# Attention over channels, then a two-layer MLP: from a schedule chosen by the compiler to one pipeline in written order

## The chip, the cores and the metric

The kernel runs on one core of one Trainium2 chip. The metric is the time of the program on the device in microseconds (us), median of several executions. TensorE has two clock levels, 1.2 and 2.4 GHz; the profile gives the granted clock as a share of the higher one. Engines are named as in the profile: PE (TensorE, with PEld for its weight loads), ACT (ScalarE), DVE (VectorE), POOL (GpSimd) and SP (SyncE, which only issues DMAs here).

## The reference

q, k and v are fp32 of shape (4, 6080, 256): four batches of 6080 tokens with 256 channels. Attention is over channels, so that its matrix is 256 x 256 for each batch; the result goes through a two-layer MLP with 2048 hidden units. tau is 1.

```python
def _attn_ref(q, k, v, tau):
    qn = q / (np.linalg.norm(q, axis=1, keepdims=True) + 1e-06)
    kn = k / (np.linalg.norm(k, axis=1, keepdims=True) + 1e-06)
    s = kn.transpose(0, 2, 1) @ qn / tau
    a = np.exp(s - s.max(-1, keepdims=True))
    a /= a.sum(-1, keepdims=True) + 1e-09
    return v @ a

def _moe_ref(x, w_in, w_out, s, b):
    r = np.maximum(x @ w_in, 0.0)
    g = s * (r * r) + b
    return g @ w_out
```

## The kernel before

**The gram.** For each batch the kernel needs the matrix k'q summed over 6080 tokens, and the sums of squares of q and k. `gram_chunks` (L104) cuts the tokens into six chunks of 1024 (the last 960). A chunk's q and k come by two DMAs from POOL's queue (L127, L131), cast from fp32 to fp16 on the way; partition p holds rows p, p+128 and so on, in runs of 1 KB in memory. ACT squares 2048 elements at a time (L147, L148), DVE folds the squares (L153 to L163), and PE adds 16 products of 256 columns to one PSUM bank (L167).

**The finish.** `gram_finish` (L178) turns the sums into norms (L180 to L190, with a reciprocal on 512 columns), scales the scores, takes the softmax (L201 to L222), transposes it (L228) and multiplies it into w_in (L237, L244). What comes out, wa16, takes v straight to the hidden layer, so that attention costs no pass of its own.

**The stream.** The 24320 tokens are cut into 48 groups of 512 (the last has 256; three groups straddle two batches). `stream_prep` (L264) loads v by POOL's queue and transposes it with eight PE transposes (L274) and a DVE copy (L278). `stream_moe` (L281) runs 16 steps m: two first-layer products of 512 columns into one of four h_ps banks (L311), a relu on ACT (L320), a square on DVE (L322), and, three steps later, four second-layer products of 256 columns into o_ps (L295), two PSUM banks that exist once. o_ps is cleared by DVE (L287) and evicted in one operation of 1024 columns (L330), which adds rowconst, the share of b, from 16 fp32 products (L99). The output leaves by SP's queue (L338).

**The order.** Nothing is pinned: the compiler's scheduler orders each engine's instructions by its own estimate of when they are ready, within what data and buffers allow. The main loop (L366) writes one chunk of the next batch's gram after each group, and the finish after the last chunk. SP loads both weights in fp32 at the start (L85, L90), ACT casts them (L87, L92). Buffers: three for a chunk's q and k, four for v, one for o_ps, four for h_ps, one more PSUM bank (ps_x) for everything else.

## Time and profile before

| | us |
|---|---|
| median of 3 runs | 905.42 |
| lowest and highest run | 902.81, 905.54 |
| span of the profiled execution | 900.5 |
| what the median has beyond that span | 4.9 |
| TensorE's recorded work in the span | 794.0 |
| VectorE's | 541.6 |
| ScalarE's | 558.2 |

The span goes from the first to the last instruction of one profiled execution. No time beside the span is recorded for that execution itself, so sums are made against the span, and the 4.9 us stand for what lies around it. In the timeline a row is one instruction, or several of a kind in a row (xN); the second number is the time from the start of the first to the end of the last, and matmuls overlap, so the pace of TensorE is read from start to start. In brackets stands the idle time ahead of the row and what ended it.

### The profile page before, as it was taken

To read this page: it belongs to the slowest core of one execution; us is meant where nothing else is said; L and a number is where in the kernel's file an instruction comes from. 1 tells how busy PE (TensorE), PEld (TensorE's weight loads), DVE (VectorE), ACT (ScalarE), POOL (GpSimd) and SP (SyncE) were. 2 spreads that over 40 slices of the span, in tenths; PEclk is the share of its full clock that TensorE was granted. 3 is DMA by queue.
4 is the path that set the end of the run, shared out by engine and by line. 5 is a ranking of instruction groups with operands and counts; after the bars stand their busy time and mean duration, and the time that the engine had idled before them with its cause. 6 is when DMAs were issued, how large, how long until landed. Compare 5 with 4: busy or idle time off the path is not lost.

```text
span 900.5 us, 14352 instructions
## 1 busy us (share of the span) xinstructions
PE 794.0 (88%) x5564; PEld 526.9 (59%) x5564; DVE 541.6 (60%) x1111; ACT 558.2 (62%) x893; POOL 85.7 (10%) x114
## 2 busy tenths in 40 slices
PE   0534799999998998778999899889999999999998
PEld 0313566666565665555566666556656666666666
DVE  1445486665766765455856676555665776565665
ACT  2864885666774655456776465556676565665665
POOL 4331300000001011111000101100000000000000
PEclk9976999999999999999999999999999999999999
DMA  9996951323026136566121713631212423230111
GB/s 230 198 197 85 197 92 36 72 38 69 24 60 105 36 71 98 80 94 94 31 48 47 107 36 69 102 62 36 60 25 47 75 44 59 48 66 25 47 41 43
DMA packets 102181, 67.38 MB, mean 75 GB/s; under 512 B 2528, under 2 KB 101856, under 8 KB 101856
## 3 DMA queue, kind: packets, MB, share of 16 engines
q0 software_dynamic: 74688, 37.36, 32.5%
q1 hardware_dynamic: 27424, 29.10, 10.1%
q8 instruction: 43, 0.70, 0.3%
q14 instruction: 26, 0.21, 0.1%
HBM read 78.91 MB, written 24.90 MB: 115 GB/s over the span
## 4 chain that ended last, share of the span: by engine, by line
PE 42%; issue 8%; DVE 4%; DMA 4%; ACT 1%; POOL 0%; ACTq 0%; POOLq 0%
PE o_ps L295 21%; PE h_ps L311 19%; DMA qc<-in_q_dram 3%; DMA kc<-in_k_dram 1%; DVE g L322 1%; ACT r L320 1%; PE vT_ps L274 1%; PE s_ps L167 1%; DVE o_sb L330 1%; DVE nrm L190 1%; PE wa_ps L237 1%; DVE o_ps L287 1%; DVE h_ps L307 0%; ACT sq L148 0%; DVE vT L278 0%
## 5 line engine op out<-in xcount | busy, mean ns | idle before, releaser
L320 ACT ACTIVATE r<-h_ps 128x512 f16<-128x512 f32 (+1 forms) x768 | 424.2, 601 | 248.1 <-PE h_ps L311 232.9
L295 PE MATMUL o_ps<-w_out,g 128*128 128x256 f16 x3040 | 426.5, 276 | 33.6 <-DVE g L322 32.8
L322 DVE TENSOR_TENSOR g<-r 128x512 f16<-128x512 f16 (+1 forms) x768 | 302.2, 418 | 223.1 <-ACT r L320 218.7
L311 PE MATMUL h_ps<-vT,wa 128*128 128x512 f16 (+7 forms) x1632 | 421.3, 370 | 0.3 <-DVE h_ps L307 0.2
L295 PEld LDWEIGHTS <-g 128*128 128x128 f16 x3040 | 290.1, 99 | 185.3 <-DVE g L322 54.9
L311 PEld LDWEIGHTS <-wa 128*128 128x128 f16 x1632 | 157.6, 99 | 83.7 <-issue 4.0
L267 POOL DMA_DIRECT2D v<-in_v_dram x48 | 36.2, 755 | 518.9 <-PE vT_ps L274 485.0
L167 PE MATMUL s_ps<-qc,kc 128*128 128x256 f16 (+1 forms) x384 | 58.4, 311 | 29.0 <-DMA kc<-in_k_dram 25.3
L147 ACT ACTIVATE sq<-qc 128x2048 f16<-128x2048 f16 x24 | 46.0, 1917 | 52.8 <-DMA qc<-in_q_dram 52.0
L330 DVE SCALAR_TENSOR_TENSOR o_sb<-o_ps,rowconst 128x1024 f32<-128x1024 f32 (+1 forms) x48 | 58.1, 1211 | 32.4 <-PE o_ps L295 32.4
L167 PEld LDWEIGHTS <-kc 128*128 128x128 f16 (+1 forms) x384 | 41.2, 111 | 43.2 <-DMA kc<-in_k_dram 28.8
L153 DVE TENSOR_TENSOR f<-sq 128x2048 f16<-128x2048 f16 x24 | 29.4, 1225 | 52.6 <-ACT sq L148 52.4
L148 ACT ACTIVATE sq<-kc 128x2048 f16<-128x2048 f16 x24 | 46.2, 1923 | 9.2 <-DMA kc<-in_k_dram 9.0
L287 DVE MEMSET o_ps<- 128x1024 f32 (+1 forms) x48 | 43.3, 903 | 10.9 <-DVE vT L278 4.7
L274 PE MATMUL vT_ps<-ident,v 128*128 128x128 f16 x380 | 32.5, 226 | 18.4 <-DMA v<-in_v_dram 16.5
L278 DVE COPY vT<-vT_ps 128x1024 f16<-128x1024 f16 (+1 forms) x48 | 32.4, 675 | 18.9 <-PE vT_ps L274 18.9
L127 POOL DMA_DIRECT2D qc<-in_q_dram x24 | 21.7, 906 | 191.2 <-issue 62.3
L274 PEld LDWEIGHTS <-v 128*128 128x128 f16 x380 | 26.4, 101 | 22.0 <-DMA v<-in_v_dram 16.7
L244 ACT ACTIVATE wa<-wa_ps,lam_sqrt_s 128x512 f16<-128x512 f32 x32 | 22.1, 692 | 8.0 <-PE wa_ps L237 7.5
L307 DVE MEMSET h_ps<- 128x512 f32 x48 | 23.3, 485 | 4.2
L131 POOL DMA_DIRECT2D kc<-in_k_dram x24 | 21.8, 909 | 8.0 <-ACT sq L148 6.8
L237 PE MATMUL wa_ps<-w_in,aT 128*128 128x512 f16 x64 | 19.4, 385 | 0.3
(48 smaller groups left out, 142.5 us busy)
## 6 DMA issues: line engine op xcount, KB each, us to landing
out_dram<-o_sb SPq DMA_DIRECT2D x47, 512.0 KB, 3.1
v<-in_v_dram POOLq DMA_DIRECT2D x47, 256.0 KB, 5.6
qc<-in_q_dram POOLq DMA_DIRECT2D x20, 512.0 KB, 9.1
kc<-in_k_dram POOLq DMA_DIRECT2D x20, 512.0 KB, 10.8
w_in<-in_moe_w_in_dram SPq DMA_DIRECT2D x1, 2048.0 KB, 10.8
w_out<-in_moe_w_out_dram SPq DMA_DIRECT2D x1, 2048.0 KB, 22.6
qc<-in_q_dram POOLq DMA_DIRECT2D x4, 448.0 KB, 8.1
kc<-in_k_dram POOLq DMA_DIRECT2D x4, 448.0 KB, 9.4
```

Source lines behind the costliest of these rows:

```text
L147: nc.scalar.activation(out=sq[:, :nsub_t, 0, :], in_=qc[:, :nsub_t, :], func=AF.Square)
L148: nc.scalar.activation(out=sq[:, :nsub_t, 1, :], in_=kc[:, :nsub_t, :], func=AF.Square)
L167: nc.tensor.matmul(s_ps[:, ch, :], kc[:nt, j, ts(ch, P)], qc[:nt, j, :], start=False, stop=False, skip_group_check=True,)
L267: nc.gpsimd.dma_start(out=v16[:, :nsub, :], in_=v_flat[t0:t1, :].rearrange("(j p) c -> p j c", p=P),)
L274: nc.tensor.transpose(vT_ps[:, ch, ts(st, P)], v16[:, st, ts(ch, P)], ident16)
L278: nc.vector.tensor_copy(out=vT16[:, :, :ntok], in_=vT_ps[:, :, :ntok])
L287: nc.vector.memset(o_ps[:, :nsub, :], 0.0)
L295: nc.tensor.matmul(o_ps[:, tsi, :], g16[:, ds(tsi * P, nt)], w_out16[:, m, :], start=False, stop=False, skip_group_check=True,)
L311: nc.tensor.matmul(h_ps[:, s0:s1], wa16[:, ci, ts(m, P)], vT16[:, ci, s0:s1], start=(simple and ci == 0), stop=(simple and ci == CH - 1), ...
L320: nc.scalar.activation(out=r16[:, :ntok], in_=h_ps[:, :ntok], func=AF.Relu)
L322: nc.vector.tensor_mul(g16[:, :ntok], r16[:, :ntok], r16[:, :ntok])
L330: nc.vector.scalar_tensor_tensor(out=o_sb[:, :nsub, :], in0=o_ps[:, :nsub, :], scalar=1.0 / (LAM * LAM), op0=ALU.mult, in1=rowconst[:, Non ...
```

## The change

Every instruction of the new main part is handed to `po`, which pins it behind the instruction written before it on its engine. The work is one loop over 768 steps (48 groups of 16): step s writes the first-layer products, relu and square of s, then the second-layer products of s-4, then the side work that is listed for s: loads and transposes of v, products and folds of the next batch's gram, its finish in 14 pieces. o_ps becomes half-banks of 2 x 256 columns, each with its own eviction, from a pool of three; a group needs two. The first product of a bank clears it, so that the memsets go. The general PSUM bank goes too: transposes, norms and folds take their turn in the four h_ps banks. q, k and v chunks are laid out so that a partition holds 8 (or 4) neighbouring rows, contiguous in memory; all six chunks of batch 0 are loaded first, then w_in, v and w_out, by POOL's queue, as fp16 (w_out a second time as fp32). DVE squares q and ACT k, in halves of 1024 elements. The k norm comes as a column from two products with a single column, so the reciprocal has 258 columns. rowconst is summed on POOL and takes one PE product. The scale s moves from wa16 to the eviction. The core of the diff:

```diff
+    def po(ins):
+        tc.keep_in_program_order(ins)
+        return ins
...
-    qk_pool = ctx.enter_context(tc.tile_pool(name="qk_pool", bufs=3))
+    qk_pool = ctx.enter_context(tc.tile_pool(name="qk_pool", bufs=6))
+    sq_pool = ctx.enter_context(tc.tile_pool(name="sq_pool", bufs=2))
     sm_pool = ctx.enter_context(tc.tile_pool(name="sm", bufs=2))
     apool = ctx.enter_context(tc.tile_pool(name="apool", bufs=2))
     vpool = ctx.enter_context(tc.tile_pool(name="vpool", bufs=4))
-    gpool = ctx.enter_context(tc.tile_pool(name="gpool", bufs=6))
-    opool = ctx.enter_context(tc.tile_pool(name="opool", bufs=3))
+    vtpool = ctx.enter_context(tc.tile_pool(name="vtpool", bufs=3))
+    rpool = ctx.enter_context(tc.tile_pool(name="rpool", bufs=3))
+    gpool = ctx.enter_context(tc.tile_pool(name="gpool", bufs=LAG + 3))
+    opool = ctx.enter_context(tc.tile_pool(name="opool", bufs=4))
     ps_gram = ctx.enter_context(tc.tile_pool(name="ps_gram", bufs=1, space=bass.MemoryType.PSUM))
-    ps_x = ctx.enter_context(tc.tile_pool(name="ps_x", bufs=1, space=bass.MemoryType.PSUM))
     ps_h = ctx.enter_context(tc.tile_pool(name="ps_h", bufs=4, space=bass.MemoryType.PSUM))
-    ps_out = ctx.enter_context(tc.tile_pool(name="ps_out", bufs=1, space=bass.MemoryType.PSUM))
+    ps_o = ctx.enter_context(tc.tile_pool(name="ps_o", bufs=3, space=bass.MemoryType.PSUM))
...
+    s_out = consts.tile([P, 1], FP32)
+    nc.vector.tensor_scalar_mul(out=s_out, in0=s_bc, scalar1=1.0 / (LAM * LAM))
...
+    JC = 8
+    chunks = []
+    at = 0
+    while at < N:
+        rows = min(P * JC, N - at)
+        assert rows % JC == 0
+        chunks.append((at, rows // JC))
+        at += rows
+    NCH = len(chunks)
+    def load_chunk(b, c):
+        at, np_ = chunks[c]
+        kc = qk_pool.tile([P, JC, C], FP16, tag="kc", name="kc")
+        qc = qk_pool.tile([P, JC, C], FP16, tag="qc", name="qc")
+        for t, src in ((kc, k), (qc, q)):
+            po(nc.gpsimd.dma_start(
+                out=t[:np_],
+                in_=src[b, at : at + np_ * JC, :].rearrange("(p j) c -> p j c", j=JC),
+            ))
+        return qc, kc
...
+            return [squares(1, 0), squares(0, 0), squares(1, 1), squares(0, 1),
+                    fold1(0), fold1(1), fold2, fold3, fold4]
...
+            def norms():
+                n_ps = ps_h.tile([P, C + CH], FP32, tag="h_ps", name="n_ps")
+                po(nc.tensor.matmul(n_ps[:, :C], ones32, self.acc[:, 0, :],
+                                    start=True, stop=False, skip_group_check=True))
                 for ch in range(CH):
+                    po(nc.tensor.matmul(n_ps[:, C + ch : C + ch + 1], self.acc[:, 1, ts(ch, P)],
+                                        ones32[:, 0:1], start=False, stop=(ch == CH - 1),
+                                        skip_group_check=True))
+                nrm = sm_pool.tile([P, C + CH], FP32, tag="nrm", name="nrm")
+                po(nc.scalar.activation(out=nrm, in_=n_ps, func=AF.Sqrt))
+                st["nrm"] = nrm
...
+            def fold_w(fo, m):
+                def f():
+                    wa_ps = ps_h.tile([P, NW], FP32, tag="h_ps", name="wa_ps")
+                    for j in range(CH):
+                        po(nc.tensor.matmul(wa_ps, st["aT"][:, j, ts(m, P)],
+                                            w_in16[:, j, ds(fo * NW, NW)],
+                                            start=(j == 0), stop=(j == CH - 1)))
+                    dst = self.wa[:, m, ds(fo * NW, NW)]
+                    if m == 0:
+                        po(nc.scalar.mul(out=dst, in_=wa_ps, mul=LAM))
+                    else:
+                        po(nc.vector.tensor_scalar_mul(out=dst, in0=wa_ps, scalar1=LAM))
+                return f
+            return [norms, recip, scores, exps, soft, a_t] + [
+                fold_w(fo, m) for fo in range(Dff // NW) for m in range(CH)]
...
+    def load_v(g):
+        t0, nj = group(g)
+        v16 = vpool.tile([P, TG // P, C], FP16, tag="v16", name="v16")
+        po(nc.gpsimd.dma_start(
+            out=v16[:, :nj, :],
+            in_=v_flat[t0 : t0 + nj * P, :].rearrange("(p j) c -> p j c", j=nj)))
+        v_tiles[g] = v16
...
-        o_ps = ps_out.tile([P, TG // P, C], FP32, tag="o_ps")
-        nc.vector.memset(o_ps[:, :nsub, :], 0.0)
...
-            r16 = gpool.tile([P, TG], FP16, tag="r16")
-            nc.scalar.activation(out=r16[:, :ntok], in_=h_ps[:, :ntok], func=AF.Relu)
-            g16 = gpool.tile([P, TG], FP16, tag="g16")
-            nc.vector.tensor_mul(g16[:, :ntok], r16[:, :ntok], r16[:, :ntok])
-            g_tiles[m] = g16
-            if m >= LAG:
-                emit_mm2(m - LAG)
-        for m in range(FT - LAG, FT):
-            emit_mm2(m)
...
+    grams = {b: Gram(b) for b in range(B)}
+    g0 = grams[0]
+    for c in range(NCH):
+        g0.load(c)
+    po(nc.gpsimd.dma_start(out=w_in16, in_=moe_w_in.rearrange("(co p) f -> p co f", p=P)))
+    load_v(0)
+    load_v(1)
+    po(nc.gpsimd.dma_start(out=w_out16, in_=moe_w_out.rearrange("(fo p) d -> p fo d", p=P)))
+    load_v(2)
+    po(nc.gpsimd.dma_start(out=w_out32, in_=moe_w_out.rearrange("(fo p) d -> p fo d", p=P)))
+    g0.start()
+    for c in range(NCH):
+        ops = g0.norm_ops(c)
+        for j in range(JC):
+            g0.mm(c, j)
+        for f in ops:
+            f()
+    fin = g0.finish_ops()
+    for f in fin[:6]:
+        f()
+    transpose_v(0)
+    for f in fin[6:]:
+        f()
+    transpose_v(1)
+    def rowconst_sum():
+        h = FT // 2
+        while h >= 1:
+            po(nc.gpsimd.tensor_add(w_out32[:, :h, :], w_out32[:, :h, :], w_out32[:, h : 2 * h, :]))
+            h //= 2
+    def rowconst_mm():
+        rc_ps = ps_h.tile([P, C], FP32, tag="h_ps", name="rc_ps")
+        po(nc.tensor.matmul(rc_ps, ones32, w_out32[:, 0, :], start=True, stop=True))
+        po(nc.vector.tensor_scalar_mul(out=rowconst, in0=rc_ps, scalar1=b_bc))
...
+    first_group = [b * N // TG for b in range(B)]
+    at_step(1, rowconst_sum)
+    at_step(12, rowconst_mm)
+    for g in range(NG):
+        if g >= 3:
+            at_step((g - 3) * FT + 2, lambda g=g: load_v(g))
+        if g >= 2:
+            at_step((g - 1) * FT + 4, lambda g=g: transpose_v(g))
+    for b in range(1, B):
+        gr = grams[b]
+        w0 = first_group[b - 1] * FT + (18 if b == 1 else 6)
+        w1 = first_group[b] * FT - 3
+        fin_len = 6 * 3 + 8 * 2
+        span = (w1 - fin_len) - w0 - 8
+        n = NCH * JC
+        for c in range(NCH):
+            sc = w0 + span * c * JC / n
+            at_step(max(3, sc - 16), lambda gr=gr, c=c: gr.load(c))
+            if c == 0:
+                at_step(sc, gr.start)
+            for j in range(JC):
+                at_step(w0 + span * (c * JC + j) / n, lambda gr=gr, c=c, j=j: gr.mm(c, j))
+            def norm_step(gr=gr, c=c, sc=sc):
+                ops = gr.norm_ops(c)
+                for i, f in enumerate(ops):
+                    at_step(int(sc) + 2 + 1 + i * 2, f)
+            at_step(sc + 1, norm_step)
+        def fin_step(gr=gr, s=w1 - fin_len):
+            ops = gr.finish_ops()
+            for i, f in enumerate(ops):
+                at_step(int(s) + 1 + (i * 3 if i < 6 else 18 + (i - 6) * 2), f)
+        at_step(w1 - fin_len, fin_step)
...
+    def mm1(s):
+        g, m = divmod(s, FT)
+        _, nj = group(g)
+        n = nj * P
+        vT = vT_tiles[g]
+        h_ps = ps_h.tile([P, TG], FP32, tag="h_ps", name="h_ps")
+        for b, p0, p1 in segments(g):
+            wa = grams[b].wa
+            for ci in range(CH):
+                if p1 - p0 == P:
+                    dst, src = h_ps[:, :n], vT[:, ci, :n]
+                else:
+                    dst = h_ps[:, :n].rearrange("f (j p) -> f j p", p=P)[:, :, p0:p1]
+                    src = vT[:, ci, :n].rearrange("f (j p) -> f j p", p=P)[:, :, p0:p1]
+                po(nc.tensor.matmul(dst, wa[:, ci, ts(m, P)], src,
+                                    start=(ci == 0), stop=(ci == CH - 1), skip_group_check=True))
+        r16 = rpool.tile([P, TG], FP16, tag="r16", name="r16")
+        po(nc.scalar.activation(out=r16[:, :n], in_=h_ps[:, :n], func=AF.Relu))
+        g16 = gpool.tile([P, TG], FP16, tag="g16", name="g16")
+        po(nc.vector.tensor_mul(g16[:, :n], r16[:, :n], r16[:, :n]))
+        g16s[s] = g16
+        if m == FT - 1:
+            del vT_tiles[g]
+    def mm2(s):
+        g, m = divmod(s, FT)
+        t0, nj = group(g)
+        g16 = g16s.pop(s)
+        for j in range(nj):
+            if m == 0 and j % 2 == 0:
+                o_halves[g, j // 2] = ps_o.tile([P, 2, C], FP32, tag="o_ps", name="o_ps")
+            po(nc.tensor.matmul(
+                o_halves[g, j // 2][:, j % 2, :], g16[:, ts(j, P)], w_out16[:, m, :],
+                start=(m == 0 and j % 2 == 0), stop=(m == FT - 1 and j % 2 == 1),
+                skip_group_check=True))
+        if m == FT - 1:
+            o_sb = opool.tile([P, TG // P, C], FP32, tag="o_sb", name="o_sb")
+            for h in range(nj // 2):
+                po(nc.vector.scalar_tensor_tensor(
+                    out=o_sb[:, 2 * h : 2 * h + 2, :], in0=o_halves.pop((g, h)),
+                    scalar=s_out, op0=ALU.mult,
+                    in1=rowconst[:, None, :].broadcast_to((P, 2, C)), op1=ALU.add))
+            po(nc.sync.dma_start(
+                out=out[t0 : t0 + nj * P, :].rearrange("(p j) d -> p j d", j=nj),
+                in_=o_sb[:, :nj, :]))
+    for s in range(NS + LAG):
+        if s < NS:
+            mm1(s)
+        if s >= LAG:
+            mm2(s - LAG)
+        for f in side.pop(s, []):
+            f()
+    assert not side
```

## Rows read from the trace of the kernel before

**Rows 1.** The page, busy time of each engine (us, share of the span, instructions)

```profile
PE 794.0 (88%) x5564; PEld 526.9 (59%) x5564; DVE 541.6 (60%) x1111; ACT 558.2 (62%) x893; POOL 85.7 (10%) x114
```

**Rows 2.** Busy time by stretch: length, five engines, TensorE clock, DMA share, GB/s

```profile
225.00:460.00 235.00, 211.23 (x1449) 136.18 (x1448) 146.48 (x299) 147.57 (x244) 20.18 (x25) 0.96 0.40 68
460.00:660.00 200.00, 186.85 (x1342) 125.53 (x1340) 125.13 (x260) 119.58 (x203) 15.60 (x20) 0.97 0.34 62
...
760.00:888.00 128.00, 128.00 (x913) 85.31 (x911) 78.79 (x170) 80.28 (x144) 2.92 (x4) 1.00 0.19 45
```

**Rows 3.** Timeline at two group boundaries: start us, us, engine, line, operation

```profile
759.46 0.61 PE L274 MATMUL vT_ps<-ident,v 128*128 128x128 f16 x8
...
759.91 3.19 PE L311 MATMUL h_ps<-vT,wa 128*128 128x512 f16 x14
...
774.32 3.19 PE L311 MATMUL h_ps<-vT,wa 128*128 128x512 f16 x14
```

**Rows 4.** Timeline of one step inside a group of the last batch

```profile
766.47 0.59 PE L311 MATMUL h_ps<-vT,wa 128*128 128x512 f16 x2
...
766.90 0.60 PE L295 MATMUL o_ps<-w_out,g 128*128 128x256 f16 x4
767.11 0.60 ACT L320 ACTIVATE r<-h_ps 128x512 f16<-128x512 f32 x1 [0.27 <-PE h_ps L311]
...
767.34 0.60 PE L311 MATMUL h_ps<-vT,wa 128*128 128x512 f16 x2
...
767.73 0.43 DVE L322 TENSOR_TENSOR g<-r 128x512 f16<-128x512 f16 x1 [0.44 <-ACT r L320]
```

**Rows 5.** Timeline around a late q chunk of batch 2

```profile
340.29 1.91 ACT L147 ACTIVATE sq<-qc 128x2048 f16<-128x2048 f16 x1 [4.27 <-DMA qc<-in_q_dram]
...
343.20 1.04 PE L295 MATMUL o_ps<-w_out,g 128*128 128x256 f16 x4 [3.59 <-DVE g L322]
...
344.02 1.06 PE L311 MATMUL h_ps<-vT,wa 128*128 128x512 f16 x2
```

**Rows 6.** Waits: who waited for whom, us in total, times, longest

```profile
PE o_ps L295 <- DVE g L322: 32.8, 13, 4.0
```

**Rows 7.** Timeline of the start: gram of batch 0, norms, rowconst

```profile
26.32 3.60 PE L167 MATMUL s_ps<-qc,kc 128*128 128x256 f16 x16 [7.76 <-DMA kc<-in_k_dram]
...
36.94 1.92 PE L167 MATMUL s_ps<-qc,kc 128*128 128x256 f16 x16 [1.67 <-DMA kc<-in_k_dram]
...
60.87 2.05 PE L180 MATMUL nrm_ps<-f3acc,ones 128*128 128x512 f32 x2 [5.28 <-DVE f3acc L163]
...
101.98 2.02 PE L167 MATMUL s_ps<-qc,kc 128*128 128x256 f16 x16 [0.46 <-DMA kc<-in_k_dram]
...
108.42 7.17 PE L99 MATMUL rc_ps<-w_out,ones 128*128 128x256 f32 x32
```

**Rows 8.** Groups by shape: count, busy us, mean ns, idle before

```profile
L156 DVE TENSOR_TENSOR f<-f 128x1024 f16<-128x1024 f16 x24 | 16.5, 688 | 0.3
L163 DVE TENSOR_TENSOR f3acc<-f3acc,f 128x512 f32<-128x512 f32 x20 | 13.8, 688 | 0.4
L190 DVE RECIPROCAL nrm<-nrm 128x512 f32<-128x512 f32 x4 | 13.4, 3352 | 0.1
...
L330 DVE SCALAR_TENSOR_TENSOR o_sb<-o_ps,rowconst 128x512 f32<-128x512 f32 x1 | 0.7, 691 | 0.5 <-PE o_ps L295 0.5
...
masks.py:199 POOL TENSOR_SCALAR_AFFINE_SELECT ident<-ident 128x128 f16<-128x128 f16 x1 | 0.3, 282 | 0.0
```

**Rows 9.** DMA issues: count, KB each, median us from issue to landing

```profile
kc<-in_k_dram POOLq DMA_DIRECT2D x20, 512.0 KB, 10.8
```

**Rows 10.** Timeline, ScalarE in the finish of batch 1

```profile
236.61 1.28 ACT L216 ACT_TABLE_LOAD   x1
...
237.90 0.51 ACT L216 ACTIVATE e_t<-st_t,rowmax 128x256 f32<-128x256 f32 x1
```

**Rows 11.** Timeline, the last eviction

```profile
896.35 0.69 DVE L330 SCALAR_TENSOR_TENSOR o_sb<-o_ps,rowconst 128x512 f32<-128x512 f32 x1 [0.49 <-PE o_ps L295]
```

## What the change will do

> **What bounds the kernel now.** I read the engines' totals first: TensorE has work recorded on 88% of the span, far more than any other engine [rows 1], so the questions are how much of that is needed and what fills the rest. The table by stretch answers it [rows 2]. From 760 to 888 us TensorE has no idle time and its clock is full; a group of 512 tokens takes 774.32 - 759.91 = 14.41 us there [rows 3]. Sixteen steps of 0.87 us (767.34 - 766.47 [rows 4]) make 13.90 and the eight transposes of v 0.45 (759.91 - 759.46 [rows 3]): the group is full, with 0.06 us lost. That is the floor of this program: a change of order gains nothing on a group without side work. The losses lie elsewhere. From 225 to 660 us TensorE is idle for 23.8 + 13.2 us and its mean clock is 0.96 to 0.97 [rows 2]. The timeline shows how: the square of a late q chunk sits on ScalarE until 340.29, the relus queue behind it, the output products wait until 343.20, and four of them then take 1.04 us in place of 0.60 [rows 4, 5], the lower of the two clock levels. By the waits, 13 such stalls cost 32.8 us [rows 6]. The third loss is the start: the rowconst products end at 115.6 us, and only then does the dense stream begin [rows 7].
>
> **The new start.** Nothing competes with batch 0's q and k any more. Chunks arrive every (36.94 - 26.32)/2 = 5.31 us [rows 7], 2.10 MB read each, or 395 GB/s; six (the last 15/16) take 31.5 us. I add 3.5 us for the first issue and landing (an estimate: the first products of before waited far longer, but behind 4 MB of weights): data complete at 35. The change's contiguous rows may do better or worse than 5.31; I take the row and keep 28 to 35 us for the six chunks.
> The Trainium skill, "DMA: Bandwidth & Descriptors", Specifications, says that runs of 512 B already reach line rate and sets the ceiling at 435 GB/s. The old runs are 1 KB and the row's 395 is 91% of that, so by the page the contiguous rows can bring at most some 3 us.
> Behind q and k, GpSimd's queue now holds w_in, v 0, v 1, w_out, v 2 and w_out once more in fp32 (the weights went through SP before, s and b go there now): 7.9 MB, 20 us at 395 GB/s. w_in is there at 40 us and used at 49, the fp16 w_out at 48 and used after step 4, the fp32 copy at 55: nothing on the path but the last, below. ScalarE's two casts of 3.6 us, gone now, lay beside the loads.
> Then a strict chain. VectorE's last squares and folds: six of 0.69 and one of at most 0.42 [rows 8], 4.6. Norm products cold, 1.7 (two passes of 512 columns took 2.05 [rows 7]; now 256 and two single columns). Square root 0.6. Reciprocal on 258 columns in place of 512: 3.35 x 258/512 = 1.7, with the add 2.0 [rows 8]. Scores and maximum 1.6, exponentials 1.2, softmax 0.9, transposes and copy 1.2 (sizes as in before). Eight folds of w_in with their evictions and two v transposes 6.7. Sum 20.5: step 0 at 55.5 us, between 50 and 62. Another 2 us go to the lower clock of the first products.
>
> **The stream.** In full-clock TensorE time: 752 steps x 0.869 + 16 half steps x 0.437 = 660; v transposes for the other 45.5 groups x 0.45 = 20.5; three grams of 96 products, 0.11 each at full clock (four of the same 256 columns start 0.43 apart between 766.90 and 767.34 [rows 4]), 31.7; three folds of 16 products of 512 columns at 0.216 (half a pair [rows 4]), 10.4; norms, small transposes and one rowconst product 4.7. Sum 727.5. Batch 1's gram is in it: its last products began at 101.98 us before, ahead of the stream [rows 7]. Fifteen of the sixteen fp32 rowconst products (7.17 us [rows 7]) go. The removed memsets of o_ps and s_ps lie on VectorE, which is 62% busy in the full stretch [rows 2]; by themselves they give nothing.
>
> **The new wait.** This is the term that I think decides the size. All instructions are pinned to the written order, and the output accumulators are three half-banks for groups that need two. Group g+1's second half needs the bank of group g's first half. Take T as the start of step s's first products, s being the step whose output products finish group g. VectorE's written order is multiply(s), eviction of half 0, eviction of half 1. From the rows [rows 4]: relu at T+0.64 (767.11 - 766.47), multiply at T+1.26 (767.73 - 766.47), so the eviction can start at about T+1.65; a 128x512 one takes 0.69 [rows 8], a pointer scalar a little more: done at T+2.4. TensorE wants the bank at T + 0.87 + 0.43 + 0.22 = T+1.52. It must wait 0.9 us, with all later products queued behind. The old schedule hid the same hand-over by issuing 14 first-layer products ahead of it [rows 3]; the strict order can't. 46 boundaries x 0.9 = 41 us. The bounds are 0 (the order or the slot comes out otherwise) and about 1.5 (eviction behind a queued fold of 0.69 as well). I take 0.9, since each summand is a row.
>
> **Side work.** Squares are cut to 1024 elements and folds spread over every second step; a step's second-layer products start 4 x 0.87 + 0.43 = 3.9 us after its first-layer ones, and its multiply ends at 1.26 + 0.43 = 1.7 [rows 4], so that 2.2 us of slack cover a fold of 0.69 or a square of about 1 us. Not covered: scores and maximum (1.6 us) fall one step ahead of a boundary in each of three batches, 1.1 each; exponentials with a table load delay relus by 2.6 us, 0.4 each. Sum 5. Loads are issued 16 steps, some 15 us, before use, and a k chunk lands 10.8 us after issue [rows 9]: covered by 4 us, nothing. If that cover goes, the stalls of [rows 5] return.
> The table load takes 1.28 us and the exponential starts 0.01 us after it [rows 10], so no more is charged. The Trainium skill, "ScalarE: Activation LUTs", What ACT_TABLE_LOAD costs, puts a switch at 2.66 us with a drain; two switches in three batches would add up to 8 us to the sum. The row speaks against the drain.
> GpSimd's sum of w_out: 3840 columns, 5.2 us by VectorE's 0.69 per 512 fp32 and 8.5 by GpSimd's own 0.282 per 128 [rows 8]. I take 8.5, its own engine. Behind it in GpSimd's queue stand v 3 and batch 1's first loads, used at step 18: with 10.8 us to land they come about 2 us late. Price 2, between 0 and 5.
>
> **Tail.** From the last eviction's start 900.5 - 896.35 = 4.2 us remain [rows 11], and 1.2 from the last product's chain ahead of it: 5.4, as before.
>
> **Sum.** 55.5 + 2 + 727.5 + 41 + 5 + 2 + 5.4 = 838 us of span, against 900.5. The median of the runs, 905.4, is 4.9 above that span; with the same around it, 843 us. About 0.3%, or 3 us, is what a measurement can tell here.
>
> **Rivals.**
> (a) The change doesn't hold the order that it writes: the hand-over is hidden, because the issue order or the slots come out otherwise than read: no boundary wait, 843 - 41 = 802. For it: before hides the same hand-over. Against: every product is pinned. Chance 0.12.
> (b) Loads arrive late and the stalls of [rows 5] persist: 32.8 us [rows 6] and the clock's shortfall, 0.04 x 235 + 0.03 x 200 = 15 [rows 2]: 843 + 48 = 891. Against: 15 us of lead. Chance 0.08.
> (c) Slower: the boundary wait drops the clock. After the wait of 3.6 us that ended at 343.20, products ran at the lower level [rows 5]; if 0.9 us each group did the same for two steps, 2 x 0.87 = 1.7 us would be added each time: 46 x 2.6 = 120, 802 + 120 = 922. Break-even is (905 - 802)/46 = 2.2 us per boundary. Against: the dense stretch keeps full clock [rows 2], and 0.9 us is a quarter of the wait that cost it. Chance 0.04.
> (d) The head isn't shortened, because loads run well below 395 GB/s or the chain is twice my price: 843 + 20 = 863. Chance 0.1.
> My forecast keeps the remaining 0.66.
>
> **How the numbers follow.** 843 us. With the head's 50 to 62, the boundary's 0.6 to 1.5 and the side work's 0 to 15, not all at one end, the forecast's own range is 822 to 880. Taking in (a) and (d) and leaving out (b) and (c) gives 800 to 880. Faster 0.94, same 0.02, slower 0.04 (only (c), and part of (b) worse than priced).
>
> **What would show it.** Right: first-layer products start near 55 us; TensorE waits 0.9 us on the eviction once per group, and groups of the last batch are 15.2 us long, longer than 14.41; clock 1.00 from 60 us on; no wait for q or k after batch 0. Wrong: groups of 14.4 us (a), relus behind a square that waits for a load (b), products of doubled duration after boundaries (c), step 0 after 62 us (d).

## The result and the profile after

The changed kernel takes 842.31 us, median of four runs (841.09 to 845.65), against 905.48 (902.81 to 909.25) for the kernel before, timed beside it: a ratio of 0.9311, 95% interval 0.9279 to 0.9344. The profiled execution has a span of 839.6 us, 60.9 less than before. The forecast was 843.

The totals of the engines, the line that answers to [rows 1]:

```profile
PE 764.9 (91%) x5542; PEld 527.6 (63%) x5542; DVE 536.5 (64%) x1134; ACT 518.3 (62%) x861; POOL 64.0 (8%) x109
```

TensorE's share rises from 88 to 91% of a shorter span, and its busy time falls by 29 us with only 22 instructions fewer. The fp32 rowconst products make 6.6 of it (7.2 us before, 0.6 after); most of the rest goes with the clock (an estimate: its mean over the span rises from 0.961 to 0.981, which is some 38 us less at the lower level, where the same products take twice as long). The table by stretch, read as [rows 2] (the last stretch is one of groups without side work):

```profile
225.00:460.00 235.00, 223.25 (x1664) 154.81 (x1663) 151.40 (x327) 151.49 (x252) 14.87 (x28) 0.99 0.36 79
460.00:660.00 200.00, 189.74 (x1395) 132.32 (x1394) 130.16 (x282) 127.93 (x213) 9.58 (x18) 0.99 0.28 64
760.00:829.00 69.00, 66.01 (x478) 45.35 (x476) 38.43 (x88) 43.78 (x75) 0.00 (x0) 1.00 0.08 32
```

From 225 to 460 us idle time halves, 23.8 to 11.8, and the clock goes from 0.96 to 0.99. From 460 to 660 it falls only from 13.2 to 10.3. The last stretch, which had no idle time before, has 3.0 us in 69. The waits name what is left (who waits for whom: us, times, longest):

```profile
PE o_ps L415 <- DVE o_sb L422: 37.5, 46, 2.0
...
PE o_ps L415 <- DVE g L403: 3.2, 2, 2.6
```

The 13 waits on the multiply [rows 6] have become two. In their place stand 46 waits on the eviction, one for each hand-over of a bank. The timeline of one of them:

```profile
814.31 0.60 ACT L401 ACTIVATE r<-h_ps 128x512 f16<-128x512 f32 x1 [0.27 <-PE h_ps L398]
...
814.95 0.42 DVE L403 TENSOR_TENSOR g<-r 128x512 f16<-128x512 f16 x1 [0.44 <-ACT r L401]
814.98 0.38 PE L415 MATMUL o_ps<-w_out,g 128*128 128x256 f16 x2
...
815.29 1.40 DVE L422 SCALAR_TENSOR_TENSOR o_sb<-o_ps,s_out,rowconst 128x512 f32<-128x512 f32 x2
816.08 0.38 PE L415 MATMUL o_ps<-w_out,g 128*128 128x256 f16 x2 [0.72 <-DVE o_sb L422]
```

VectorE is idle for 0.44 us ahead of the multiply, waiting for its relu, while the eviction that TensorE wants stands behind that multiply in the written order. The two output products at 814.98 go into the third bank; the next two need the bank that the first of the two evictions empties. They are late by 0.72 us.

The start answers to [rows 7]:

```profile
11.12 3.57 PE L128 MATMUL s_ps<-qc,kc 128*128 128x256 f16 x16 [11.12 <-DMA qc<-in_q_dram]
...
35.64 1.91 PE L128 MATMUL s_ps<-qc,kc 120*128 120x256 f16 x16 [1.56 <-DMA qc<-in_q_dram]
40.21 0.98 PE L191 MATMUL n_ps<-acc,ones 128*128 128x256 f32 x2 [2.66 <-DVE acc L180]
...
53.91 2.32 PE L398 MATMUL h_ps<-vT,wa 128*128 128x512 f16 x10
```

A chunk comes every (35.64 - 11.12)/5 = 4.90 us, 428 GB/s, and the first steps begin at 53.91. Just behind them is a loss that the prediction had at the wrong size, in the same timeline:

```profile
55.17 12.12 DVE L403 TENSOR_TENSOR g<-r 128x512 f16<-128x512 f16 x10 [0.22 <-ACT r L401]
...
56.59 9.26 POOL L320 TENSOR_TENSOR w_out<-w_out 128x2048 f32<-128x2048 f32 x4 [24.39 <-DMA w_out<-in_moe_w_out_dram]
...
58.24 0.59 PE L398 MATMUL h_ps<-vT,wa 128*128 128x512 f16 x2
61.44 1.03 PE L415 MATMUL o_ps<-w_out,g 128*128 128x256 f16 x4 [2.60 <-DVE g L403]
61.47 0.60 ACT L401 ACTIVATE r<-h_ps 128x512 f16<-128x512 f32 x1 [3.74 <-DVE g L403]
```

For as long as GpSimd adds up w_out (9.26 us), ten multiplies of 0.42 us take 12.12 us; relus and products queue behind them, and the products that follow take 1.03 in place of 0.60, the lower clock.

### The profile page after: what moved, and what is told of

The parts are those of the page before. It is cut to its first block, busy times and chain, and to the rows that moved or that the text cites. A ratio compares the mean times of both kernels' runs of the same rounds, so it can differ in the third digit from the quotient of the medians.

```text
span 839.6 us, 14219 instructions
## 1 busy us (share of the span) xinstructions
PE 764.9 (91%) x5542; PEld 527.6 (63%) x5542; DVE 536.5 (64%) x1134; ACT 518.3 (62%) x861; POOL 64.0 (8%) x109
## 4 chain that ended last, share of the span: by engine, by line
PE 76%; DMA 7%; DVE 7%; ACT 4%; issue 3%; POOL 1%; POOLq 0%; ACTq 0%
PE o_ps L415 35%; PE h_ps L398 34%; DMA qc<-in_q_dram 4%; DVE o_sb L422 4%; ACT r L401 4%; PE s_ps L128 3%; DMA w_out<-in_moe_w_out_dram 3%; PE vT_ps L286 2%; DVE g L403 2%; PE wa_ps L252 1%; POOL w_out L320 1%; DVE nrm L204 1%; ACT sq L152 0%; DVE sm_s L210 0%; DVE f L161 0%
## 5 line engine op out<-in xcount | busy, mean ns | idle before, releaser
L401 ACT ACTIVATE r<-h_ps 128x512 f16<-128x512 f32 (+1 forms) x768 | 450.4, 592 | 278.6 <-PE h_ps L398 243.9
L403 DVE TENSOR_TENSOR g<-r 128x512 f16<-128x512 f16 (+1 forms) x768 | 329.8, 431 | 279.0 <-ACT r L401 271.9
L415 PE MATMUL o_ps<-w_out,g 128*128 128x256 f16 x3040 | 467.6, 274 | 40.7 <-DVE o_sb L422 37.5
L398 PE MATMUL h_ps<-vT,wa 128*128 128x512 f16 (+7 forms) x1632 | 456.3, 367 | 0.0
L422 DVE SCALAR_TENSOR_TENSOR o_sb<-o_ps,s_out,rowconst 128x512 f32<-128x512 f32 x95 | 66.7, 743 | 0.5 <-PE o_ps L415 0.5
L152 ACT ACTIVATE sq<-kc 128x1024 f16<-128x1024 f16 (+1 forms) x48 | 49.7, 1048 | 21.2 <-DMA kc<-in_k_dram 21.2
L149 DVE TENSOR_TENSOR sq<-qc 128x1024 f16<-128x1024 f16 (+1 forms) x48 | 32.4, 685 | 9.4 <-DMA qc<-in_q_dram 9.4
L161 DVE TENSOR_TENSOR f<-sq 128x1024 f16<-128x1024 f16 (+1 forms) x48 | 32.4, 685 | 0.2
L168 DVE TENSOR_TENSOR f<-f 128x1024 f16<-128x1024 f16 (+1 forms) x24 | 16.4, 685 | 0.2
L180 DVE TENSOR_TENSOR acc<-acc,f 128x512 f32<-128x512 f32 (+1 forms) x20 | 13.7, 686 | 0.2
L103 POOL DMA_DIRECT2D kc<-in_k_dram x24 | 13.3, 553 | 5.1 <-DMA kc<-in_k_dram 5.0
L103 POOL DMA_DIRECT2D qc<-in_q_dram x24 | 13.2, 551 | 4.2 <-DMA qc<-in_q_dram 3.8
```

The costliest lines, as they stand in the source:

```text
L149: po(nc.vector.tensor_mul(st["sq"][:np_, 0, js, :], qc[:np_, js, :], qc[:np_, js, :]))
L152: po(nc.scalar.activation(out=st["sq"][:np_, 1, js, :], in_=kc[:np_, js, :], func=AF.Square))
L161: po(nc.vector.tensor_add(st["f1"][:np_, a], sq[:np_, a, : JC // 2, :], sq[:np_, a, JC // 2 :, :]))
L398: po(nc.tensor.matmul(dst, wa[:, ci, ts(m, P)], src, start=(ci == 0), stop=(ci == CH - 1), skip_group_check=True))
L401: po(nc.scalar.activation(out=r16[:, :n], in_=h_ps[:, :n], func=AF.Relu))
L403: po(nc.vector.tensor_mul(g16[:, :n], r16[:, :n], r16[:, :n]))
```

## The experiments

All are edits of the kernel after. Its 842.31 us is what each is held against. The kernel before, timed beside each of them, took 902.82 to 905.48 us, so the ratio to it (0.9311 for the kernel after) stands with each. Where a waiting line is quoted, it is from the waits of the profile.

**1. The eviction ahead of the multiply.** The multiply is taken out of mm1 into a function of its own, and the evictions out of mm2:

```diff
             mm2(s - LAG)
+            evict(s - LAG, 0)
+        if s < NS:
+            mul(s)
+        if s >= LAG:
+            evict(s - LAG, 1)
```

> The eviction of a group's first half is written ahead of that step's multiply, in place of behind it; nothing else moves. Theory (TensorE waits once per group because the eviction stands behind the multiply in VectorE's order): the 43 waits of 0.72 us that stand apart from a batch's finish go, 31 us, and the three of 2.03 us stay at 1.3 or more, since scores and maximum are still ahead: 842 - 31 = 811 us, groups without side work of 14.4 to 14.5 us. Rival 1 (the pause is only where TensorE's lead over ScalarE and VectorE is given back, and the loss moves to other waits): 830 to 842 us, with as much waiting elsewhere. Rival 2 (the multiply, now 0.3 us later, holds output products four steps on): waits on the multiply appear, over 842.

Measured: 809.18 us, ratio 0.8967 (0.8936 to 0.8997). The waits:

```profile
PE o_ps L421 <- DVE o_sb L435: 6.7, 9, 1.7
```

Nine waits are left, three of them the 1.70 us at a batch's finish. First evictions in the last batch:

```profile
767.28 0.75 DVE L435 SCALAR_TENSOR_TENSOR o_sb<-o_ps,s_out,rowconst 128x512 f32<-128x512 f32 x1
...
781.76 0.75 DVE L435 SCALAR_TENSOR_TENSOR o_sb<-o_ps,s_out,rowconst 128x512 f32<-128x512 f32 x1
```

A group takes 14.48 us (781.76 - 767.28). The theory holds, with 33 us less by the medians and 31 by the ratios: the wait came from the place of two instructions in VectorE's order, and no other wait takes what it gave up.

**2. Four half-banks.**

```diff
-name="ps_h", bufs=4 ... name="ps_o", bufs=3
+name="ps_h", bufs=3 ... name="ps_o", bufs=4
```

A half-bank holds one half of a group's output, 128 x 512 in fp32, as much as one of the first layer's banks; the two pools have seven together in every variant.

> Four half-banks for the output and three for the first layer, in place of three and four. Theory (the wait is for the third bank to come round): no wait of TensorE on an eviction, the three long ones included: 842 - 37.5 = 805 us. Rival (with three first-layer banks the relus set the pace where a square of 1.05 us or a table load of 1.28 us stands ahead of them): new waits on relus, 815 us or more; 842 if they take all of it.

Measured: 797.04 us, ratio 0.8833 (0.8803 to 0.8864), 45.3 less than the kernel after (43 by the ratios) and 8 below the expectation. No wait of TensorE on an eviction is left, and three first-layer banks cost next to nothing (0.7 us of waits on relus). The gain is larger than the 37.5 us that the waits summed to, and the pace tells why. The evictions of two groups in the last batch, first of the kernel after, then of this one:

```profile
800.07 1.40 DVE L422 SCALAR_TENSOR_TENSOR o_sb<-o_ps,s_out,rowconst 128x512 f32<-128x512 f32 x2
...
815.29 1.40 DVE L422 SCALAR_TENSOR_TENSOR o_sb<-o_ps,s_out,rowconst 128x512 f32<-128x512 f32 x2
```

```profile
742.15 1.40 DVE L422 SCALAR_TENSOR_TENSOR o_sb<-o_ps,s_out,rowconst 128x512 f32<-128x512 f32 x2
756.49 1.41 DVE L422 SCALAR_TENSOR_TENSOR o_sb<-o_ps,s_out,rowconst 128x512 f32<-128x512 f32 x2
```

A group takes 15.22 us with three banks and 14.34 with four: 0.88 a boundary, of which the trace shows 0.72 as waiting (ends of products are modelled). 46 x 0.88 = 40.5; the three finish boundaries waited 2.03 - 0.72 = 1.3 longer, 3.9: together 44.4 of the 45.3.

**3. Two half-banks.** The same lines with 5 and 2.

> Two half-banks for the output and five for the first layer: the hand-over wait made longer. Theory (each boundary waits for the eviction and for nothing else, and the clock stays): the first half of the next group now waits some 1.05 us for the first eviction and the second another 0.45 for the second, 1.5 in place of 0.72, 46 x 0.8 = 36 us: 878 us, clock 0.98. Rival (the prediction's rival on the clock: a wait of this length drops the clock, as three finish waits of 2.03 us did twice at 412 and 614 us): some 1.5 us more at each boundary, up to 46 x 1.5 = 70 on top, about 950 us, products at doubled duration after boundaries.

Measured: 873.5 us, ratio 0.9682 (0.9649 to 0.9714). A boundary in the last batch:

```profile
767.43 0.38 PE L415 MATMUL o_ps<-w_out,g 128*128 128x256 f16 x2 [0.94 <-DVE o_sb L422]
...
768.09 0.38 PE L415 MATMUL o_ps<-w_out,g 128*128 128x256 f16 x2 [0.28 <-DVE o_sb L422]
```

Two waits, 0.94 and 0.28, and a clock of 1.00 after them. The next group's eviction of the first half starts at 782.51, this group's at 766.63, so that a group takes 15.88 in place of 15.22, and 46 x 0.66 = 30: the time goes up by 31 us, as the lengthened wait alone would have it, and the rival's 950 falls. But the rival's mechanism is there at longer waits. In the kernel after, at the finish of batch 2:

```profile
411.63 0.38 PE L415 MATMUL o_ps<-w_out,g 128*128 128x256 f16 x2 [2.03 <-DVE o_sb L422]
...
412.89 1.06 PE L415 MATMUL o_ps<-w_out,g 128*128 128x256 f16 x4
413.75 1.06 PE L398 MATMUL h_ps<-vT,wa 128*128 128x512 f16 x2
...
416.14 0.60 PE L415 MATMUL o_ps<-w_out,g 128*128 128x256 f16 x4
```

**4. The row sum on TensorE.** The fp32 copy of w_out, its load and GpSimd's adds go; rowconst is summed from the fp16 copy.

```diff
-        po(nc.tensor.matmul(rc_ps, ones32, w_out32[:, 0, :], start=True, stop=True))
+        for m in range(FT):
+            po(nc.tensor.matmul(rc_ps, ones16, w_out16[:, m, :],
+                                start=(m == 0), stop=(m == FT - 1)))
-    at_step(1, rowconst_sum)
```

> GpSimd's four adds of w_out and the fp32 copy of w_out are gone; the sum over rows is made by sixteen fp16 products with ones at step 12 (it takes the fp16 copy of w_out, so rowconst is the sum of rounded values). Theory (the adds hold VectorE's multiplies up for as long as they run; from 58.24 to 67.99 us four steps took 9.75 in place of 3.48): 6.3 us less, sixteen products of 0.11 in place of two of 0.30, 1.2 more: 842 - 5 = 837 us, multiplies of 0.42 from the first on, no wait on a multiply near 60 us. Rival 1 (the loads of batch 1 are what is late there, as the prediction had it): the same stalls, 843. Rival 2 (the start is slow because the products are cold): doubled products up to 67 us all the same, 843.

Measured: 837.57 us, ratio 0.9264 (0.9240 to 0.9288). From the first products of step 0 to the first eviction it takes 73.71 - 55.39 = 18.32 us, in the kernel after 77.50 - 53.91 = 23.59: 5.3 less, and 1.3 of added products are in it, so the adds had cost 6.6. (Step 0 itself begins 1.5 later: the sixteen products that fold w_in take 5.61 us in place of 4.33, longer at the lower clock.) Products run at full clock from step 0 on:

```profile
57.55 0.60 PE L410 MATMUL o_ps<-w_out,g 128*128 128x256 f16 x4
...
61.02 0.60 PE L410 MATMUL o_ps<-w_out,g 128*128 128x256 f16 x4
```

Both rivals (late loads, cold products) fall.

**5. The sum a second time.**

```diff
     at_step(12, rowconst_mm)
+    at_step(612, rowconst_sum)
```

> The four GpSimd adds run a second time, on the same tile after its last use, in the last batch (GpSimd comes to them near 580 us): the suspected cost doubled. Theory (adds starve the multiplies, wherever they run): some 6 us more, 848, multiplies stretched over about 9 us and waits of TensorE on a multiply there. Rival (a matter of the start alone: clock, loads): 842 within 0.3%, nothing stretched near the second adds.

Measured: 849.35 us, ratio 0.9389 (0.9363 to 0.9416). GpSimd came to the adds at 669 us, not 580, in a stretch where nothing else changes:

```profile
668.99 9.29 POOL L320 TENSOR_TENSOR w_out<-w_out 128x2048 f32<-128x2048 f32 x4
```

The first of the adds and the first two of the multiplies by themselves, and the products that wait for them:

```profile
668.99 4.52 POOL L320 TENSOR_TENSOR w_out<-w_out 128x2048 f32<-128x2048 f32 x1
...
669.25 4.56 DVE L404 TENSOR_TENSOR g<-r 128x512 f16<-128x512 f16 x1 [0.37 <-ACT r L402]
673.73 2.56 DVE L404 TENSOR_TENSOR g<-r 128x512 f16<-128x512 f16 x1
...
673.86 0.61 PE L416 MATMUL o_ps<-w_out,g 128*128 128x256 f16 x4 [1.81 <-DVE g L404]
...
676.35 1.03 PE L416 MATMUL o_ps<-w_out,g 128*128 128x256 f16 x4 [1.44 <-DVE g L404]
```

The add ends at 673.51, the multiply that began 0.26 us into it at 673.81; the next multiply is held behind the second add in the same way, and products go to the lower clock (1.03). The picture of the start repeats 600 us later, for 7 us: it is the adds and not the start.

**6. Memsets in place of the second adds.** `nc.gpsimd.memset` over the same four sizes, at the same place in the queue.

> As the repeated sum, but the four operations that GpSimd runs a second time, near 670 us and over the same 2048, 1024, 512 and 256 columns, are memsets: GpSimd writes the tile and reads nothing. Theory (a multiply of VectorE, with two operands in SBUF, waits for a GpSimd add to end because the add reads SBUF too; 3 to 4 multiplies were held until 673.86, 676.35 and 677.75, the ends of the adds): no multiply stretched, 842 within 0.3%, against 849 with the adds. Rival (any long work of GpSimd holds VectorE up): the same stretch over as long as the memsets run, up to 849 us.

Measured: 842.32 us, ratio 0.9315 (0.9289 to 0.9341).

```profile
667.57 3.78 POOL L325 MEMSET w_out<- 128x2048 f32 x4
```

```profile
667.84 0.43 DVE L408 TENSOR_TENSOR g<-r 128x512 f16<-128x512 f16 x1 [0.37 <-ACT r L406]
668.71 0.42 DVE L408 TENSOR_TENSOR g<-r 128x512 f16<-128x512 f16 x1 [0.44 <-ACT r L406]
669.58 0.43 DVE L408 TENSOR_TENSOR g<-r 128x512 f16<-128x512 f16 x1 [0.44 <-ACT r L406]
```

These multiplies start while GpSimd is busy, and none is stretched. The memsets are shorter (3.78 us against 9.29), but the first of the adds held a multiply that began 0.26 us into it. So GpSimd that only writes doesn't hold VectorE up here; GpSimd that reads two tensors does. One that reads a single tensor was not tried.

**7. q and k rows strided again.** `"(p j) c -> p j c"` becomes `"(j p) c -> p j c"`.

> q and k rows laid on partitions with a stride again, as in the kernel before (runs of 1 KB in place of 8 KB); nothing else. Theory (the layout only shortens the six chunks of the start, 4.9 us each in place of 5.31): step 0 some 2.5 us later, at 56.4, and nothing in the stream, where chunks are issued 40 us or more before use: 845 us. Rival 1 (the row of before was slowed by other loads, the layout gives nothing): 842 within 0.3%, step 0 at 54. Rival 2 (more packets, longer issues on GpSimd and longer landings reach the stream): 847 or more, waits for q or k after batch 0.

Measured: 846.58 us (841.86, the profiled run, to 847.5), ratio 0.9351 (0.9326 to 0.9375). The chunks start from 11.48 to 39.15, 5.53 us each, close to the 5.31 of [rows 7]; step 0 begins at 57.73, 3.8 later than in the kernel after. No wait for q or k appears behind batch 0, though GpSimd now takes 0.91 us an issue in place of 0.55. The layout is worth some 3 to 4 us, all of it at the start. The profiled run is the fastest of its six because the clock dropped at none of its three finishes, where it dropped at two in the kernel after; its mean is 0.984, that of the other five 0.974 to 0.977.

**8. Weights ahead of q and k.** The loads of w_in and the fp16 w_out are moved ahead of `g0.load`.

> w_in and the fp16 w_out are issued ahead of batch 0's q and k in GpSimd's queue; nothing else. Theory (the start is bound by the loads in the order of the queue): 4.2 MB at the 2.10 MB in 4.9 us of the chunks, 9.8 us, all of it ahead of step 0: first steps at 63.7, 852 us; the order of the loads is then a fifth to a sixth of the start's gain over the kernel before, whose dense stream began at 115.6. Rival (loads share the rings, so weights ahead of them only take part of the time, or the chain behind the data is what counts): step 0 at 54 to 58, 842 to 846.

Measured: 852.16 us, ratio 0.9424 (0.9389 to 0.9459): the expected 10 us. The last chunk's first product is 10.6 later (46.24 against 35.64). But the first steps begin at 70.81, not 63.7. The adds fell into the softmax chain this time:

```profile
57.27 9.05 POOL L320 TENSOR_TENSOR w_out<-w_out 128x2048 f32<-128x2048 f32 x4 [19.48 <-DMA w_out<-in_moe_w_out_dram]
...
57.93 6.40 DVE L233 TENSOR_SCALAR a<-sm_e,sum__337 128x256 f16<-128x256 f32 x2
```

Two scalings that take 0.61 us in the kernel after took 6.40, and the multiplies behind them were then free: the first eviction is at 87.82, 10.3 later than after. The cost of the adds moved, it didn't grow.

**9. A lead of 4 steps for the loads.** `sc - 16` becomes `sc - 4`.

> q and k chunks of batches 1 to 3 are written 4 steps ahead of use in place of 16. Theory from the trace after (a step only sets the place in GpSimd's queue; GpSimd runs ahead until a v load waits for its buffer, so that chunks of batch 2 were issued at 196 and 214 us and squared at 252 and 275): real lead 40 us or more, so that 12 steps less leave over 25 us: 842 within 0.3%, no wait for q or k. Rival, the prediction's own step (lead is 16 steps, some 15 us, and the cover 4 us): with 3.5 us of lead and 7.7 to 10.1 us to land, 18 chunks late by 4 to 6 us, 70 us or more, 910 us.

Measured: 841.91 us, ratio 0.9306 (0.9271 to 0.9341). Batch 2's first chunk was issued at 213.39 us and squared at 251.87: 38 us of lead with 4 steps written. No wait for q or k appears behind batch 0. GpSimd isn't held to the step at which a load is written; it goes down its queue until a v load waits for a buffer.

**10. Nothing pinned.** The call in `po` is taken out.

> The same program with no instruction pinned to the written order. Theory (the written order is only safe because it is held; left free, the scheduler hides the hand-over as the kernel before did, and may bring its stalls back): no wait of 0.72 us at boundaries, 31 us less, and some stalls of TensorE on multiplies, up to the 48 us that they cost in the kernel before: 811 to 860 us. Rival 1 (pinning changes nothing, the order comes out as written): 842 within 0.3%. Rival 2 (the gain of the change is the pinning): 860 us or more.

Measured: 857.18 us, ratio 0.9503 (0.9464 to 0.9541), inside the theory's wide range, but most of the loss is at the start. ScalarE there:

```profile
59.87 2.00 ACT L151 ACTIVATE sq<-kc 128x1024 f16<-128x1024 f16 x2 [11.20 <-DMA kc<-in_k_dram]
...
61.78 1.06 ACT L256 ACTIVATE wa<-wa_ps 128x512 f16<-128x512 f32 x2
...
62.41 1.87 PE L251 MATMUL wa_ps<-w_in,aT 128*128 128x512 f16 x4 [8.17 <-ACT wa L256]
```

A square of batch 1 was put ahead of the evictions of batch 0's folds and waited 11.20 us for its k chunk. Step 0 began at 67.48, 13.6 later. Over the whole stream the two orders are worth about the same: waits on evictions fall from 37.5 to 13.3 us (8 are left of 46), and waits on multiplies rise from 3.2 to 13.3. They differ by stretch. From 460 to 850 us the free order has no idle time on TensorE; before that, ScalarE's squares of batches 1 to 3 wait for their k chunks, 36.0 us in 15 times behind step 0, and never in the pinned order. So what pinning buys here is that no square stands on ScalarE ahead of its load, and what it costs is the hand-over.

**11. Three parts undone at once** (nothing pinned, strided rows, weights first).

> Three parts of the change undone at once: nothing pinned, q and k rows strided, weights issued ahead of batch 0's q and k. Alone they cost 15, 4 and 10 us. Theory (they are separate losses and add up): 842 + 29 = 871 us, and the other 32 us up to the kernel before belong to what stays changed (work cut smaller and spread, row sum off TensorE, half-banks). Rival (they hide one another: late weights and late chunks fall into the same waits at the start): 855 to 865. Rival 2 (a free order with late loads brings back all of the old stalls): 890 or more.

Measured: 883.55 us, ratio 0.9775 (0.9759 to 0.9792): 41 us, where the three alone add up to 29, between the theory's 871 and the second rival's 890: the sum is larger than its parts. The start, where step 0 begins at 80.58, looks worse than in any other run:

```profile
57.96 4.50 POOL L319 TENSOR_TENSOR w_out<-w_out 128x2048 f32<-128x2048 f32 x1 [12.02 <-DMA w_out<-in_moe_w_out_dram]
62.41 0.92 POOL L102 DMA_DIRECT2D qc<-in_q_dram  x1
```

```profile
68.00 2.93 PE L127 MATMUL s_ps<-qc,kc 128*128 128x256 f16 x13 [11.69 <-DMA qc<-in_q_dram]
71.78 0.29 PE L240 MATMUL t_ps<-ident,a 128*128 128x128 f16 x1 [0.85 <-DVE a L232]
```

The q load of batch 1 stands behind an add that waits for the fp32 w_out, and the gram of batch 1 ahead of batch 0's transposes: TensorE waits 11.69 us for data that it doesn't need yet. But the extra isn't there: step 0 is 26.7 us later than in the kernel after, and the three alone move it by 13.6, 3.8 and 16.9 (experiments 10, 7 and 8). It lies behind step 0. The same work of TensorE, read as [rows 2], takes 796.42 us here and 783.02 in experiment 10, 13.4 less (the second row):

```profile
80.58:877.00 796.42, 745.60 (x5389) 510.06 (x5386) 484.54 (x1065) 492.04 (x832) 48.18 (x71) 0.98 0.33 66
```

```profile
67.48:850.50 783.02, 745.81 (x5404) 510.21 (x5402) 489.22 (x1074) 494.78 (x835) 39.75 (x75) 0.99 0.31 69
```

The longest idle time of TensorE in it is that of [rows 5], a square that waits for its chunk, with relus queued behind it:

```profile
142.33 1.06 ACT L151 ACTIVATE sq<-kc 128x1024 f16<-128x1024 f16 x1 [5.91 <-DMA kc<-in_k_dram]
...
143.92 1.01 PE L397 MATMUL h_ps<-vT,wa 128*128 128x512 f16 x2 [3.79 <-ACT r L400]
```

The squares' waits for k behind step 0 go from 36.0 us in experiment 10 to 44.0. So a part of the old stalls is back, as the second rival had it, though not all. Undoing these three gives back two thirds of the change's 63 us; which of the remaining parts hold the other 20 was not taken apart.

**12. The two gains together** (experiments 2 and 4).

> Four output half-banks and three for the first layer, and the row sum by fp16 products with ones (the two edits that gained alone). Theory (they are different losses, the boundary and the GpSimd adds): 797 - 5 = 792 us. Rival (with three first-layer banks the start's pile of relus is held by them in place of the adds, so the second gain is lost in part): 794 to 797.

Measured: 791.47 us (791.12 to 791.77), ratio 0.8753 (0.8727 to 0.8778), the fastest of all.

```profile
55.00:70.00 15.00, 14.99 (x106) 10.14 (x105) 7.96 (x19) 9.84 (x18) 1.27 (x3) 1.00 0.87 171
70.00:784.00 714.00, 712.16 (x5304) 499.07 (x5302) 478.85 (x1055) 487.72 (x819) 38.21 (x72) 1.00 0.33 73
```

From 55 to 784 us TensorE is idle for 1.9 us, at full clock. What is left is the start and the products themselves.

## Why the prediction was right

- **Start.** 55.5 predicted, 53.91 found. Six chunks: 5.31 taken, 4.90 found; data complete at 35, and the last chunk's first product at 35.64. That these two agree is luck in part: the first issue and landing took 11.12 - 4.90 = 6.2 us where 3.5 were added, and the quicker chunks made up for it. The part of the start behind the data took 53.91 - 35.64 = 18.3, priced at 20.5; the folds of w_in with the transposes of v are most of the difference (4.6 from 49.29 to 53.91, priced at 6.7). The change of layout is worth 3 to 4 us (experiment 7). The Trainium skill, "DMA: Bandwidth & Descriptors", Specifications, sets a ceiling of 435 GB/s; 428 was found, and the bound of some 3 us that was worked out from it was right in size. What the Trainium skill has there of 512 B, that they are enough for line rate, is not borne out: runs of 1 KB (512 B once they are fp16) gave 2.10 MB in 5.53 us, 379 GB/s.
- **Cold first products, 2 us.** Not found as such: in experiment 4 every product from step 0 on runs at full clock. The lower clock near 62 us belongs to the adds.
- **The new wait**, the term that decided the size: 0.9 predicted, 0.88 by the pace and 0.72 as recorded, 46 times. The row-by-row reading was right in its order and in who waits, and experiments 1 to 3 move it at will: removed by another order, removed by a bank, lengthened by taking one. Groups of 15.2 us were predicted and 15.22 found.
- **Side work, 5 us.** Found: 3 x 1.3 for scores and maximum (3.3 predicted), and 1.7 for each drop of the clock that followed, two in the profiled run (from 412.29 to 416.57 three steps took 4.28 in place of 2.61). Together 7.3; the clock was not in the term, and its sign (1.00 from 60 us on) is the one that didn't come. The exponential began 0.01 us behind its table load of 1.28 (214.02, 215.31), so that nothing was to be added. The Trainium skill, "ScalarE: Activation LUTs", What ACT_TABLE_LOAD costs, has a drain in its 2.66; the trace shows none.
- **The loads' cover.** "Some 15 us" of lead, "covered by 4": wrong, though the price of nothing was right. The lead of batch 2's first chunk is 38 us even with 4 steps written (experiment 9). The step that failed is taking a place in the written order as a time; GpSimd runs ahead of it.
- **GpSimd's sum, 2 us (0 to 5).** The duration was right (8.5 predicted, 9.26 found), the mechanism wrong. It was priced by what stands behind it in GpSimd's queue; batch 1's first chunk was issued late indeed (66.38) and came just in time. What it cost is 6.6 us, through VectorE, which was named nowhere in the step (experiments 4 to 6). The Trainium skill, "SBUF — State Buffer", Who interferes with whom, has the rule: a VectorE instruction with two inputs in SBUF contends with a GpSimd instruction that reads SBUF, not with one that only writes, and the later one waits until the earlier ends. The runs agree: held for 4.56 us behind an add of 4.52, free beside memsets.
- **The sum.** 838 predicted as a span and 839.6 found. The start came out 1.6 and the cold products 2 below their price, the boundaries (40.5) 0.5; side work 2.3 and GpSimd 4.6 above; the rest is spread. Wrong terms of opposite sign lie inside a good total, so that its closeness is luck in part; the term that decides the size is not. The 4.9 us added to the span were misread as what lies around it: for the profiled run of the kernel after the whole time is recorded too, 841.44, which is 1.8 above its span. Some 3 of the 4.9 were the spread between executions, so that the time to hold 842.31 against is 840 and not 843.
- **The rivals.** (a) is false for this kernel, and experiment 2 shows its price: 43 to 45 us, 41 predicted. (b) is false, by a wider margin than argued. (c) is false at waits of 0.72 and of 0.94 us; the drop that it feared comes at the finishes, after 13 of 24 waits of 2.03 to 2.25 us (last section). (d) is false; experiments 8 and 11 show what would have made it true. What (b) feared came back in experiments 10 and 11, where the order was free.

## What to carry to other kernels

When every instruction is pinned, read the order of the engine that frees a buffer: here two adjacent instructions of VectorE, one of them waiting for its input, were worth 31 to 33 us, and one more bank 43 to 45. An operation that is put on an idle engine isn't free by that; price it by what it shares with the busy ones, and look at the busy engine's durations while it runs. A program's written place for a load is an upper bound on its issue time if its queue can run ahead.

## What the runs showed of the hardware

- **VectorE beside GpSimd.** While GpSimd's tensor add ran (4.5, 2.4, 1.3 and 0.8 us for 2048 to 256 fp32 columns), a VectorE multiply of 0.42 us that started during an add ended some 0.3 us behind it (4.56 us beside an add of 4.52); scalings from fp32 were held the same way (two took 6.40 in place of 0.61 us). Beside memsets of 3.78 us nothing was held.
- **The clock after a wait.** Over eight kernels (the one after, and experiments 3 to 9) there are 24 waits of 2.03 to 2.25 us at a batch's finish, ahead of which TensorE was busy at full clock. After 13 of them the granted clock fell to some 0.6 over the next 4 us, after 11 it stayed at 1.00. After the three waits of 1.70 us in experiment 1, and after the hand-over waits of 0.72 and 0.94 us, it stayed at 1.00. In experiment 5 two waits of 1.81 and 1.44 us, which ended at 673.86 and 676.35 beside the second adds, were followed by the lower clock. The number of drops goes with the span: 836.2 us in experiment 9 with none, 839.6 in the kernel after with two, 841.8 in experiment 6 with three.
- **Idle time as recorded and as lost.** 0.72 us of waiting cost 0.88 us of pace, so a sum of waits on products, whose ends are modelled, was a fifth too low here.
